# Reordering the setup of a fused long-convolution and SwiGLU kernel, gating its weight loads, and splitting a pair of transposes

## The chip, the cores and the metric

The kernel runs on one core of one Trainium2 chip. The metric is the device time of one execution in microseconds (us); lower is better. The profile is one execution recorded by the hardware profiler; its span is a little shorter than the device time (346.7 us against a median of 349.8 us for the kernel before). PE is the TensorE matmul engine, DVE is VectorE, ACT is ScalarE, POOL is GpSimd, SP issues the DMAs (46 of 48 in the trace of the kernel before).

## The reference, cut to what matters

```python
# x: [1, 2048, 640] bf16.  State space of 192 complex modes per channel; F = 1536
h  = x + A(layernorm(x))             # A: long convolution + skip
h2 = h + B(layernorm(h))             # B: SwiGLU

def A(u):                            # per channel d
    K[d, l] = Re sum_n C[d,n] * exp(dt[d] * A[d,n] * l) * dt[d] * B[d,n]
    y = causal convolution of u with K along l (by FFT)
    return y + u * Dskip
def B(x):
    return (silu(x @ w1) * (x @ w3)) @ w2
```

The kernel builds the convolution filter for three chunks of channels (256, 256 and 128), transforms it with small matmuls, and then convolves block by block: 8 token chunks of 256 tokens, each with a forward transform, a product with the filter's spectrum `kf`, and an inverse transform, followed by the SwiGLU.

## The kernel before

The kernel asks for a manual schedule (`tc.manual_schedule()`), and in its traces each engine's instructions stand in the order in which the Python code issues them: that order is the schedule. The setup has, for each channel chunk h, two tables `at` and `bt` (ACT computes sines and exponentials, DVE multiplies them up), a product `k_mm` of the two on PE, its drain `k_evac` on ACT, and a transform `k_dft` on PE, whose result ACT copies to `kf` (for the last chunk ACT and DVE):

```python
    def k_dft(h, kc):                      # 256 small matmuls, each with its own weight load
        pp = [ps2("g"), ps2("g")]
        for i in range(II):                # 16
            for f in range(NFT):           # 4
                for blk in range(4):
                    ...
                    T.matmul(ob, lhsT=wt[...], rhs=rb, ...)
        return pp
    ...
    pb = k_dft(0, kc)
    kf_evac(0, pb, "SSSS")                 # ACT
    for ig, st in zip(IGS, stg):
        b_mul(1, bt1, "sin", ig, st)       # DVE
    zs2 = z_sin(2)                         # ACT: 6 sines
    bt2 = b_tile(2)
    b_first(2, bt2, "sin")                 # ACT: 30 sines
    stg = [b_rest(2, bt2, "exp", ig) for ig in IGS]    # ACT: 15 exponentials
    ...                                    # DVE: a_chain(2), b_mul(2)
    warm(14, last_a(1, at1))               # PE: matmuls whose result nobody reads
    warm(10, last_b(1, bt1, 1))
    for b in range(nb[1]):                 # 4 blocks
        pk = k_mm(1, at1, bt1, kc, b)      # PE
        k_evac(1, pk, kc, b)               # ACT: behind all of chunk 2's sines and exponentials
    ...
    nc.sync.dma_start(out=w1sb[:], ...)    # 1.97 MB each, issued as soon as their space is free
    nc.sync.dma_start(out=w3sb[:], ...)
    pb = k_dft(1, kc)
    kf_evac(1, pb, "SSSS")
    inverse_table()                        # 8 transposes on PE, then a copy to gt on DVE
    warm(8, last_b(2, bt2, 0))
    ...                                    # k_mm(2), k_evac(2)
    lst[0] = ln1_stats(0, V)               # DVE: mean, variance, 1/sqrt by Newton steps
    ulns[0] = ln1_apply(0, lst[0])
    lst[1] = ln1_stats(1, G)               # the Newton steps on POOL
    for f in range(NFT):
        fwd_evac(0, f, fwd_mm(ulns[0], f)) # forward transform of token chunk 0 -> vt
    pb = k_dft(2, kc)
    ...                                    # DVE: skip(0), apply(1), stats(2), skip(1), stats(3)
    kf_evac(2, pb, "SVSV")
```

The loop over token chunks, with `gu` a gate/up pair of matmul groups (20 matmuls, six times a pass):

```python
        gu(c, 4)
        if n1:
            tp = ps2("d", BF16)
            for k in range(2):
                tr_mm(c + 1, k, tp)        # 5 transposes on PE into PSUM tile tp
                tr_evac(c + 1, k, tp)      # ACT copies them to xt; PE's second half waits for it
        run(pr, 1)
        gu(c, 5)
        run(pr, 1)
        po = out_mm(c, 0)
        ...
```

Of the kernel before, what the change touches and what calls it, by code (L numbers as in the profile page):

```python
# [14 lines left out]
NFT = 4  # L15
# [13 lines left out]
def kernel(  # L29
# [105 lines left out]
    def inverse_table():  # L135
        tp = ps2("d", BF16)
        for i in range(NFT):
            for kt in range(2):
                T.transpose(out=tp[:, 0, i * TB + kt * P:i * TB + kt * P + P], in_=ft[:, kt, i * P:(i + 1) * P], identity=ident[:])
        V.tensor_copy(out=gt[:], in_=tp[:, 0, :].rearrange("p (i t) -> p i t", i=NFT))  # L140

    dtl = kp.tile([P, D], BF16, name="dtl")
    S.activation(out=dtl[:], in_=ldb[:], func=ACT.Exp)
# [96 lines left out]
    def b_nsin(h, i, dst):  # L240
        S.activation(out=dst, in_=grp(h, 1), func=ACT.Sin, scale=-float(i))  # L241

    def b_first(h, bt, kind):
        bv = b_view(h, bt)
        for i in range(1, II):
            if kind == "exp":
                b_exp(h, i, bv[:, 0, :, i, :])
            else:
                b_cos(h, i, bv[:, 0, :, i, :])
                b_nsin(h, i, bv[:, 1, :, i, :])  # L250
# [113 lines left out]
    def run(gen, n=None):  # L364
        r = None
        while n is None or n > 0:
            try:
                r = next(gen)
            except StopIteration:
                break  # L370
            if n is not None:
                n -= 1
        return r

    def rstd(v, n, eng):
        va = small.tile([P, 2], F32, name="va")
        ta = small.tile([P, 2], F32, name="ta")
        rs = small.tile([P, 2], F32, name="rs")
        u, t, r = va[:, 0:n], ta[:, 0:n], rs[:, 0:n]
        V.tensor_scalar(out=u, in0=v, scalar1=EPS, scalar2=None, op0=ALU.add)  # L380
        V.tensor_single_scalar(out=t.bitcast(I32), in_=u.bitcast(I32), scalar=1, op=ALU.arith_shift_right)
        V.tensor_scalar(out=r.bitcast(I32), in0=t.bitcast(I32), scalar1=-1.0, scalar2=float(0x5F3759DF), op0=ALU.mult, op1=ALU.add)  # L382
        for _ in range(2):
            eng.tensor_tensor(out=t, in0=r, in1=r, op=ALU.mult)  # L384
            eng.tensor_tensor(out=t, in0=t, in1=u, op=ALU.mult)
            eng.tensor_scalar(out=t, in0=t, scalar1=-0.5, scalar2=1.5, op0=ALU.mult, op1=ALU.add)
            eng.tensor_tensor(out=r, in0=r, in1=t, op=ALU.mult)
        return rs

    def bn(mv, k, src):  # L390
        st = small.tile([P, 2, V.BN_STATS_DIM], F32, name="st")
        for q in range(2):
            V.bn_stats(out=st[:, q, :], in_=src[:, q * (D // 2):(q + 1) * (D // 2)])  # L393
        V.bn_aggr(out=mv[:, k, :], in_=st[:])

    def ln1_stats(c, eng):
        mv = small.tile([P, 2, 2], F32, name="mv")
        for k in range(2):
            bn(mv, k, xs[:, 2 * c + k, :])
        return mv, rstd(mv[:, :, 1], 2, eng)  # L400

    def ln1_apply(c, stats):
        mv, rs = stats
        uln = vp.tile([P, 2, D], BF16, name="uln", bufs=2)
        for k in range(2):
            V.tensor_scalar(out=uln[:, k, :], in0=xs[:, 2 * c + k, :], scalar1=mv[:, k, 0:1], scalar2=rs[:, k:k + 1],
                            op0=ALU.subtract, op1=ALU.mult)
        return uln

# [4 lines left out]

    vts = {}

    def fwd_mm(uln, f):
        pv = ps2()
        for k in range(2):
            for q in range(2):  # L420
                T.matmul(pv[:, q, 0:D // 2], lhsT=ft[:, k, f * P:(f + 1) * P],  # L421
                         rhs=uln[:, k, q * (D // 2):(q + 1) * (D // 2)], start=(k == 0), stop=(k == 1))
        return pv

    def fwd_evac(c, f, pv):
        if f == 0:
            vts[c] = vp.tile([P, 2, 2, D], BF16, name="vt", bufs=4)
        S.copy(out=vts[c][:, f // 2, f % 2, :].rearrange("p (q d) -> p q d", q=2), in_=pv[:, :, 0:D // 2])  # L428

    w_mul(0, 0)  # L430
    alpha(0)
# [43 lines left out]
    z_mul(1, zs1, ze1)  # L475
    run(a_chain(1, at1, zs1))
    pb = k_dft(0, kc)
    kf_evac(0, pb, "SSSS")
    for ig, st in zip(IGS, stg):
        b_mul(1, bt1, "sin", ig, st)  # L480
    zs2 = z_sin(2)
    bt2 = b_tile(2)
    b_first(2, bt2, "sin")
    stg = [b_rest(2, bt2, "exp", ig) for ig in IGS]
    z_mul(2, zs2, ze2)
    at2 = kp.tile([P, 2 * JJ * CWM], BF16, name="at", bufs=1)
    V.tensor_copy(out=a_view(2, at2)[:, :, :, 0, :], in_=wl2[:].rearrange("p a (q c) -> p a q c", c=2))
    run(a_chain(2, at2, zs2))
    for ig, st in zip(IGS, stg):
        b_mul(2, bt2, "exp", ig, st)  # L490
    warm(14, last_a(1, at1))
    warm(10, last_b(1, bt1, 1))
    kc = kp.tile([P, II * 4 * 2 * (max(CHUNKS) // 8)], BF16, name="kc")
    for b in range(nb[1]):
        pk = k_mm(1, at1, bt1, kc, b)
        k_evac(1, pk, kc, b)
    bctx.close()
    wts = ctx.enter_context(tc.tile_pool(name="wts", bufs=1, side="right", reuse_waits="tile"))
    w1sb = wts.tile([P, DT, F], BF16, name="w1sb")
    w3sb = wts.tile([P, DT, F], BF16, name="w3sb")  # L500
    vp = ctx.enter_context(tc.tile_pool(name="vp", bufs=4, side="right", reuse_waits="tile"))
    nc.sync.dma_start(out=w1sb[:], in_=B_w1.rearrange("(s p) f -> p s f", p=P))
    nc.sync.dma_start(out=w3sb[:], in_=B_w3.rearrange("(s p) f -> p s f", p=P))
    pb = k_dft(1, kc)
    kf_evac(1, pb, "SSSS")
    inverse_table()
    kc = kp.tile([P, II * 4 * 2 * (max(CHUNKS) // 8)], BF16, name="kc")
    warm(8, last_b(2, bt2, 0))
    for b in range(nb[2]):
        pk = k_mm(2, at2, bt2, kc, b)  # L510
        k_evac(2, pk, kc, b)
    lst, ulns = {}, {}
    lst[0] = ln1_stats(0, V)
    ulns[0] = ln1_apply(0, lst[0])
    lst[1] = ln1_stats(1, G)
    for f in range(NFT):
        fwd_evac(0, f, fwd_mm(ulns[0], f))
    pb = k_dft(2, kc)
    skip(0, ulns[0])
    ulns[1] = ln1_apply(1, lst[1])  # L520
    lst[2] = ln1_stats(2, G)
    skip(1, ulns[1])
    lst[3] = ln1_stats(3, G)
    kf_evac(2, pb, "SVSV")
    kctx.close()
    if dbg and "kf" in dbg:
        nc.sync.dma_start(out=dbg["kf"], in_=kf[:])

    mp = ctx.enter_context(tc.tile_pool(name="mp", bufs=1, side="left", reuse_waits="tile"))
    w2sb = mp.tile([P, FT, D], BF16, name="w2sb")  # L530
    nc.sync.dma_start(out=w2sb[:], in_=B_w2.rearrange("(s p) d -> p s d", p=P))
    zz, xx, hst, xls, xts = {}, {}, {}, {}, {}

    def product(c):
# [3 lines left out]
        x = z if c == 0 else mp.tile([P, 2, 2, D], BF16, name="xf", bufs=2)  # L538
        zz[c], xx[c] = z, x
        zp = zz.pop(c - 1, None)  # L540
        pstr = z[:].ap[0][0]
        n = D // 2
        for q in range(2):
            r = slice(q * n, (q + 1) * n)
# [10 lines left out]
                                        op=(ALU.subtract if a == e else ALU.add))  # L555
            yield

    def inv_mm(c, k):
        py = ps2()
        for f in range(NFT):  # L560
            for q in range(2):
                T.matmul(py[:, q, 0:D // 2], lhsT=gt[:, f, k * P:(k + 1) * P],  # L562
                         rhs=xx[c][:, f // 2, f % 2, q * (D // 2):(q + 1) * (D // 2)], start=(f == 0), stop=(f == NFT - 1))
        return py

    def h_add(c, k, py):
        hv = xs[:, 2 * c + k, :].rearrange("p (q d) -> p q d", q=2)
# [50 lines left out]
                        in1=xs[:, tt, :].rearrange("p (q d) -> p q d", q=2), op=ALU.add)  # L618
        nc.sync.dma_start(out=out_view[:, tt, :], in_=ot[:])

    run(product(0))
    for f in range(NFT):
        fwd_evac(1, f, fwd_mm(ulns[1], f))
    py = [inv_mm(0, 0), inv_mm(0, 1)]
    for k in range(2):
        h_add(0, k, py[k])
        rs = rstd(hst[0][:, k:k + 1, 1], 1, V)
        ln2_apply(0, k, hst[0], rs, 0)
        tp = ps2("d", BF16)
        tr_mm(0, k, tp)  # L630
        tr_evac(0, k, tp)
        if k == 0:
            ulns[2] = ln1_apply(2, lst[2])
            for f in range(NFT):
                fwd_evac(2, f, fwd_mm(ulns[2], f))
    run(product(1))
    skip(2, ulns[2])

    for c in range(NC):
        n1, n2, n3, n4 = (c + 1 < NC), (c + 2 < NC), (c + 3 < NC), (c + 4 < NC)  # L640
        if n3:
            ulns[c + 3] = ln1_apply(c + 3, lst[c + 3])
        gu(c, 0)
        if n1:
            p0 = inv_mm(c + 1, 0)
            h_add(c + 1, 0, p0)
        gu(c, 1)
        if n1:
            p1 = inv_mm(c + 1, 1)
            h_add(c + 1, 1, p1)  # L650
            rs = rstd(hst[c + 1][:, :, 1], 2, G)
        gu(c, 2)
        if n3:
            for f in (0, 1):
                fwd_evac(c + 3, f, fwd_mm(ulns[c + 3], f))
            skip(c + 3, ulns[c + 3])
        gu(c, 3)
        if n1:
            for k in range(2):
                ln2_apply(c + 1, k, hst[c + 1], rs, k)  # L660
        if n3:
            for f in (2, 3):
                fwd_evac(c + 3, f, fwd_mm(ulns[c + 3], f))
        pr = product(c + 2) if n2 else iter(())
        if n4:
# [19 lines left out]
_INS = ['A_u', 'A_A_re', 'A_A_im', 'A_B_re', 'A_B_im', 'A_C_re', 'A_C_im', 'A_log_dt', 'A_Dskip', 'B_x', 'B_w1', 'B_w3', 'B_w2']  # L685
# [26 lines left out]
```

## Time and profile before

| | before |
|---|---|
| median, range | 349.8 us, 348.0 to 352.0 (16 runs) |
| span of the profiled run | 346.7 us |
| busy PE / DVE / ACT / POOL | 74 / 78 / 43 / 11 % |

Those shares are averages over two quite different stretches. The first view is the table of busy time by stretch, with the cuts at 99.2 us (DVE has finished the last table, `bt2`) and at 151.3 us (start of the second gate/up group). Its columns are the stretch, its length, busy time of each engine (with instruction counts), the mean granted PE clock as a share of full speed, the DMA share and GB/s.

```profile
0.00:99.20 99.20, 39.72 (x620) 27.86 (x621) 93.85 (x166) 84.27 (x191) 3.27 (x14) 0.86 0.26 70
99.20:151.30 52.10, 31.53 (x695) 20.84 (x695) 37.46 (x115) 16.24 (x27) 9.45 (x24) 0.74 0.33 115
151.30:346.70 195.40, 184.95 (x1580) 151.60 (x1577) 140.40 (x309) 49.31 (x81) 26.58 (x88) 1.00 0.04 15
```

Up to 99.2 us DVE is busy for 93.9 us of 99.2: it bounds that part, and the change leaves its work there alone. From 151.3 us PE is busy for 185 of 195 us at full clock: it bounds the loop. Between lie 52.1 us in which no engine is the limit: DVE works for 37.5 us of it, PE for 31.5, and the PE clock averages 0.74. That stretch is where a better order can win.

The next view is the chain of waits in that stretch: start, length, and the work or wait that held up everything behind it.

```profile
97.98 0.24 PE ps L308 x8
...
98.24 1.50 ACT kc L326 x2
...
99.79 2.16 PE ps L336 x242
101.95 4.90 issue
106.85 0.39 PE ps L336 x14
107.24 0.98 PE ps L139 x8
...
108.24 0.69 DVE gt L140
108.93 0.80 DVE st L393 x2
```

DVE could have gone on at 99.24 us. It waits until 108.24 because its next instruction, the copy of `gt`, hangs on PE's `k_dft(1)`, which begins only at 99.79 and stops for 4.90 us in the middle ("issue": the engine waited for nothing that the trace records). The list of DVE's waits from 49 to 135 us (engine, line, what it waited for; total us, times, longest) shows that wait as the largest:

```profile
DVE gt L140 <- PE ps L139: 9.0, 1, 9.0
DVE uln L406 <- POOL rs L387: 1.7, 1, 1.7
DVE xs L568 <- PE ps L562: 1.7, 1, 1.7
```

What is PE doing in those 4.90 us? The DMA view of 104 to 106 us shows two queues at work (packets, MB, share of the 16 DMA engines' time):

```profile
q1 hardware_dynamic: 267, 0.77, 99.8%
q8 instruction: 1, 0.02, 3.3%
```

q8, which the profile calls "instruction", moves packets of 16 KB (22 packets, 0.36 MB in the whole run), and they keep PE's pace: in the loop eleven of them begin from 156.28 us up to, but not including, the one at 328.10, and PE starts 2820 matmuls and weight loads in that time, 256 for each packet. At 256 each, 22 packets make 5632 instructions, and PE has 5784 matmuls and weight loads. From this the author takes q8 as the fetch of PE's instructions. In this trace one such packet begins between 104 and 106 us (at 104.29, by the packet records of the trace, and it ends at 105.35), and none between 98 and 104, while the loads of `w1` and `w3`, issued at 98.28 and 98.71 us, keep the DMA engines nearly full.

In the loop the wait between the two halves of the transpose shows in PE's timeline (start, length, line, operation, operands, count; in brackets the idle time before it and what ended it):

```profile
188.96 0.44 PE L581 MATMUL ps<-ident,xl 128*128 128x128 bf16 x5
190.39 0.44 PE L581 MATMUL ps<-ident,xl 128*128 128x128 bf16 x5 [0.99 <-DVE ta L381]
190.66 1.25 PE L597 MATMUL ps<-xt,w1sb 128*128 128x256 bf16 x10
191.75 1.25 PE L597 MATMUL ps<-xt,w3sb 128*128 128x256 bf16 x10
192.84 6.68 PE L610 MATMUL ps<-w2sb,hm 128*128 128x320 bf16 x48
```

PE stands still for 0.99 us while ACT empties the first half (the trace names a DVE instruction as the one that ended the wait in this pass, and ACT's `xt` copy in four of the seven; ACT's copy ends at the same moment, and `xt` is what the code makes it wait for).

### The profile page before, as it was taken

What the parts mean: (1) busy time and instruction counts of PE and PEld (TensorE: products, weight loads), DVE (VectorE), ACT (ScalarE), POOL (GpSimd) and SP (SyncE); (2) the same over time, 40 slices, a digit from 0 to 9 for tenths busy, and PEclk for the clock granted to TensorE, in tenths of its full rate; (3) what the DMA queues carried; (4) which work ended last, traced back from release to release, by engine and by line L of the source; (5) the groups of instructions that cost most, each with busy time, mean ns of one, the idle gap of its engine ahead of it and who ended that gap; (6) DMA issues with size and microseconds to landing.
All of it is one profiled execution on the core that took longest, in us unless ns stands there. A gap on an engine that the chain in (4) does not pass through costs nothing.

```text
span 346.7 us, 7002 instructions
## 1 busy us (share of the span) xinstructions
PE 256.2 (74%) x2892; PEld 200.3 (58%) x2892; DVE 271.7 (78%) x588; ACT 149.8 (43%) x298; POOL 39.3 (11%) x126
## 2 busy tenths in 40 slices
PE   3303056377256655788998998998998998998995
PEld 1201025254254432467787787787787787787884
DVE  6899999999944797999888798798796685873331
ACT  2999999939931630425115115116015023022120
POOL 2000000000000352003303203203202001010000
PEclk9999999558786965699999999999999999999999
DMA  5823800000057070000000000000000000100101
GB/s 158 265 89 92 182 0 2 0 6 1 0 185 275 2 227 5 0 1 2 20 20 2 19 21 0 22 19 2 21 19 2 20 21 0 41 2 0 40 0 38
DMA packets 10655, 15.74 MB, mean 45 GB/s; under 512 B 1536, under 2 KB 9216, under 8 KB 10496
## 3 DMA queue, kind: packets, MB, share of 16 engines
q1 hardware_dynamic: 10336, 15.11, 14.0%
q8 instruction: 22, 0.36, 0.4%
q10 hardware_dynamic: 288, 0.20, 0.2%
q14 instruction: 9, 0.07, 0.1%
HBM read 12.42 MB, written 2.88 MB: 44 GB/s over the span
## 4 chain that ended last, share of the span: by engine, by line
PE 55%; DVE 24%; ACT 13%; issue 4%; DMA 1%; POOL 1%; SPq 0%; DVEq 0%
PE ps L597 28%; PE ps L610 15%; PE ps L562 5%; DVE st L393 4%; ACT bt L241 2%; ACT kc L326 2%; PE ps L421 2%; DVE at L291 2%; DVE tt L293 2%; DVE at L296 2%; PE ps L308 2%; PE ps L336 2%; ACT bt L238 1%; ACT stg L238 1%; ACT sg L602 1%
## 5 line engine op out<-in xcount | busy, mean ns | idle before, releaser
L602 ACT ACTIVATE sg<-ps 128x512 bf16<-128x512 f32 x48 | 28.7, 597 | 133.5 <-PE ps L597 133.5
L597 PE MATMUL ps<-xt,w1sb 128*128 128x256 bf16 x480 | 60.2, 273 | 1.1 <-ACT xt L586 1.1
L597 PE MATMUL ps<-xt,w3sb 128*128 128x256 bf16 x480 | 60.2, 273 | 0.0
L603 DVE TENSOR_TENSOR hm<-sg,ps 128x512 bf16<-128x512 bf16 x48 | 32.9, 686 | 33.4 <-ACT sg L602 33.0
L610 PE MATMUL ps<-w2sb,hm 128*128 128x320 bf16 x384 | 53.5, 299 | 0.0
L597 PEld LDWEIGHTS <-w1sb 128*128 128x128 bf16 x480 | 46.7, 98 | 8.1 <-issue 1.2
L597 PEld LDWEIGHTS <-w3sb 128*128 128x128 bf16 x480 | 47.0, 98 | 5.4
L610 PEld LDWEIGHTS <-hm 128*128 128x128 bf16 x384 | 37.6, 98 | 14.2
L384 POOL TENSOR_TENSOR ta<-rs 128x2 f32<-128x2 f32 x28 | 8.9, 317 | 203.1 <-DVE rs L382 202.0
L393 DVE BATCH_NORM_STATS2 st<-xs 128x6 f32<-128x320 bf16 x64 | 27.9, 478 | 0.5
L308 PE MATMUL ps<-bt,at 128*128 128x128 bf16 (+1 forms) x320 | 18.8, 239 | 10.6 <-ACT kc L326 10.5
L617 DVE TENSOR_TENSOR ot<-ps,xs 128x640 bf16<-128x640 f32 x16 | 13.2, 825 | 15.7 <-PE ps L610 15.7
L421 PE MATMUL ps<-uln,ft 128*128 128x320 bf16 x128 | 23.2, 332 | 2.0 <-ACT kc L326 0.8
L308 PEld LDWEIGHTS <-at 128*128 128x128 bf16 (+1 forms) x320 | 16.5, 106 | 13.5 <-issue 11.4
L428 ACT CAST vt<-ps 128x640 bf16<-128x640 f32 x32 | 21.0, 694 | 4.2 <-PE ps L421 4.2
L562 PEld LDWEIGHTS <-gt 128*128 128x128 bf16 x128 | 13.1, 103 | 13.4 <-DVE z L549 4.5
L241 ACT ACTIVATE bt<-alp 128x384 bf16<-128x384 f32 (+1 forms) x45 | 20.6, 458 | 0.0
L356 PEld LDWEIGHTS <-ident 128*128 128x128 bf16 x56 | 7.0, 132 | 23.4 <-DVE at L296 12.0
L291 DVE TENSOR_TENSOR at<-at,zs 128x1536 bf16<-128x1536 bf16 (+3 forms) x30 | 20.2, 675 | 0.1
L293 DVE TENSOR_TENSOR tt<-at,zs 128x1536 bf16<-128x1536 bf16 (+3 forms) x30 | 20.2, 673 | 0.0
L336 PE MATMUL ps<-kc,wt 32*128 32x64 bf16 (+1 forms) x768 | 8.8, 204 | 14.5 <-issue 8.4
L296 DVE TENSOR_TENSOR at<-at,tt 128x1536 bf16<-128x1536 bf16 (+3 forms) x30 | 19.1, 678 | 0.5
(96 smaller groups left out, 371.4 us busy)
## 6 DMA issues: line engine op xcount, KB each, us to landing
xs<-in_A_u_dram SPq DMA_DIRECT2D x4, 640.0 KB, 6.3
out_dram<-ot SPq DMA_DIRECT2D x16, 160.0 KB, 1.8
wt<-ftd SPq DMA_DIRECT2D x4, 512.0 KB, 7.7
w1sb<-in_B_w_dram SPq DMA_DIRECT2D x1, 1920.0 KB, 8.6
w3sb<-in_B_w_dram SPq DMA_DIRECT2D x1, 1920.0 KB, 13.1
w2sb<-in_B_w_dram SPq DMA_DIRECT2D x1, 1920.0 KB, 9.5
ftd<-ft SPq DMA_DIRECT2D x1, 256.0 KB, 2.1
par_ar<-in_A_A_re_dram SPq DMA_DIRECT2D x2, 96.0 KB, 3.8
```

What stands on the lines that cost most here:

```text
L241: S.activation(out=dst, in_=grp(h, 1), func=ACT.Sin, scale=-float(i))
L291: V.tensor_tensor(out=av[:, part, :, o0:o0 + w, :], in0=src, in1=z4[:, 0].broadcast_to([P, cw // 2, w, 2]), op=ALU.mult)
L293: V.tensor_tensor(out=tv[:, part], in0=src, in1=z4[:, 1].broadcast_to([P, cw // 2, w, 2]), op=ALU.mult)
L296: V.tensor_tensor(out=dst, in0=dst, in1=tv[:, 1 - part], op=(ALU.add if part else ALU.subtract))
L308: T.matmul(pk[:, half, gi * P:(gi + 1) * P], lhsT=at[r, c], rhs=bt[r, c], start=first, stop=last, tile_position=((r.start, 0) if n1 else N ...
L393: V.bn_stats(out=st[:, q, :], in_=src[:, q * (D // 2):(q + 1) * (D // 2)])
L421: T.matmul(pv[:, q, 0:D // 2], lhsT=ft[:, k, f * P:(f + 1) * P], rhs=uln[:, k, q * (D // 2):(q + 1) * (D // 2)], start=(k == 0), stop=(k = ...
L562: T.matmul(py[:, q, 0:D // 2], lhsT=gt[:, f, k * P:(k + 1) * P], rhs=xx[c][:, f // 2, f % 2, q * (D // 2):(q + 1) * (D // 2)], start=(f == ...
L597: T.matmul(pg[:, b, u * TB:(u + 1) * TB], lhsT=w[:, kt, fb * P:(fb + 1) * P], rhs=xts[c][:, kt, :], start=(kt == 0), stop=(kt == DT - 1))
L602: S.activation(out=sg[:], in_=pg[:, 0, :], func=ACT.Silu)
L603: V.tensor_tensor(out=hms[c][:, 2 * fp:2 * fp + 2, :], in0=sg[:].rearrange("p (u t) -> p u t", u=2), in1=pg[:, 1, :].rearrange("p (u t) -> ...
L610: T.matmul(po[:, q, 0:D // 2], lhsT=hms[c][:, fb, k * P:(k + 1) * P], rhs=w2sb[:, fb, q * (D // 2):(q + 1) * (D // 2)], start=(fb == 0), s ...
```

## The change

Its intent is to shorten the stretch from 99 to 151 us, and to fill the wait in the loop. It has six parts:

1. ACT's order: chunk 2's sines run while PE is in `k_dft(0)`, and chunk 2's exponentials alternate with the drains of chunk 1.
2. The loads of w1 and w3 are gated: SP first issues a tiny DMA out of the last `kf`, so that they start after the last `k_dft`.
3. The transposes go on either side of the sixth gate/up group.
4. DVE's layernorm work is reordered: statistics of token chunks 0 and 1 together with one shared 1/sqrt; the two halves of chunk 0 share one in the second layernorm too; the forward transforms run two chunks ahead instead of three, so one moves from the setup into the loop.
5. Fewer warm-up matmuls (30 instead of 56).
6. `gt`, and the whole of the last `kf`, is copied by ACT instead of DVE; the forward transform is split by halves of the channels, and the inverse one too, so that products can begin earlier; ACT's first Silu stands ahead of the loop, and with it the table load of 1.28 us that the trace shows before it.

The diff, cut to its core:

```diff
@@ inverse_table
-        V.tensor_copy(out=gt[:], in_=...)
+        S.copy(out=gt[:], in_=...)
@@ setup
     pb = k_dft(0, kc)
-    kf_evac(0, pb, "SSSS")
     ...
     zs2 = z_sin(2)
     bt2 = b_tile(2)
-    b_first(2, bt2, "sin")
-    stg = [b_rest(2, bt2, "exp", ig) for ig in IGS]
+    b_first(2, bt2, "sin", 1, 8)
+    kf_evac(0, pb, "SSSS")
+    b_first(2, bt2, "sin", 8, II)
     ...
-    warm(14, last_a(1, at1))
-    warm(10, last_b(1, bt1, 1))
+    warm(6, last_b(1, bt1, 1))
+    stg = []
     for b in range(nb[1]):
         pk = k_mm(1, at1, bt1, kc, b)
+        if b < len(IGS):
+            stg.append(b_rest(2, bt2, "exp", IGS[b]))
         k_evac(1, pk, kc, b)
     ...
-    nc.sync.dma_start(out=w1sb[:], ...)
-    nc.sync.dma_start(out=w3sb[:], ...)
     pb = k_dft(1, kc)
     ...
-    warm(8, last_b(2, bt2, 0))
     ...
-    lst[0] = ln1_stats(0, V); ulns[0] = ln1_apply(0, lst[0]); lst[1] = ln1_stats(1, G)
-    for f in range(NFT):
-        fwd_evac(0, f, fwd_mm(ulns[0], f))
     pb = k_dft(2, kc)
-    ...   # skip(0), apply(1), stats(2), skip(1), stats(3)
-    kf_evac(2, pb, "SVSV")
+    mv, ulns = ln1_stats((0, 1)), {}
+    rs = rstd(mv[:, :, 1], 4, V)
+    ...   # apply(0), apply(1), stats(2), skip(0), skip(1)
+    kf_evac(2, pb, "SSSS")
+    for q, part in ((0, 0), (0, 1), (1, 0), (1, 1)):
+        fwd(0, ulns[0], q, part)
+    warms = small.tile([P, 1], F32, name="warms")
+    S.activation(out=warms[:], in_=pit[:], func=ACT.Silu)
     ...
+    gate(kf[0:1, 1, 1, D - 64:D])          # SP: tiny DMA that waits for the last kf
+    nc.sync.dma_start(out=w1sb[:], ...)
+    nc.sync.dma_start(out=w3sb[:], ...)
     nc.sync.dma_start(out=w2sb[:], ...)
@@ loop
         gu(c, 4)
         if n1:
             tp = ps2("d", BF16)
-            for k in range(2):
-                tr_mm(c + 1, k, tp)
-                tr_evac(c + 1, k, tp)
+            tr_mm(c + 1, 0, tp)
+            tr_evac(c + 1, 0, tp)
         run(pr, 1)
         gu(c, 5)
+        if n1:
+            tr_mm(c + 1, 1, tp)
+            tr_evac(c + 1, 1, tp)
         run(pr, 1)
     ...   # ln1_apply and the forward transform of chunk c + 2 instead of c + 3
```

More of the change, by code (lines that the diff above doesn't have):

```diff
@@ L139, in inverse_table @@
                 T.transpose(out=tp[:, 0, i * TB + kt * P:i * TB + kt * P + P], in_=ft[:, kt, i * P:(i + 1) * P], identity=ident[:])
-        V.tensor_copy(out=gt[:], in_=tp[:, 0, :].rearrange("p (i t) -> p i t", i=NFT))
+        S.copy(out=gt[:], in_=tp[:, 0, :].rearrange("p (i t) -> p i t", i=NFT))
     dtl = kp.tile([P, D], BF16, name="dtl")
@@ L241, in b_nsin, with b_first @@
         S.activation(out=dst, in_=grp(h, 1), func=ACT.Sin, scale=-float(i))
-    def b_first(h, bt, kind):
+    def b_first(h, bt, kind, i0=1, i1=II):
         bv = b_view(h, bt)
-        for i in range(1, II):
+        for i in range(i0, i1):
             if kind == "exp":
@@ L375, in rstd @@
     def rstd(v, n, eng):
-        va = small.tile([P, 2], F32, name="va")
-        ta = small.tile([P, 2], F32, name="ta")
-        rs = small.tile([P, 2], F32, name="rs")
+        va = small.tile([P, 4], F32, name="va")
+        ta = small.tile([P, 4], F32, name="ta")
+        rs = small.tile([P, 4], F32, name="rs")
         u, t, r = va[:, 0:n], ta[:, 0:n], rs[:, 0:n]
@@ L394, in bn, with ln1_stats, ln1_apply @@
         V.bn_aggr(out=mv[:, k, :], in_=st[:])
-    def ln1_stats(c, eng):
-        mv = small.tile([P, 2, 2], F32, name="mv")
-        for k in range(2):
-            bn(mv, k, xs[:, 2 * c + k, :])
-        return mv, rstd(mv[:, :, 1], 2, eng)
-    def ln1_apply(c, stats):
-        mv, rs = stats
-        uln = vp.tile([P, 2, D], BF16, name="uln", bufs=2)
-        for k in range(2):
-            V.tensor_scalar(out=uln[:, k, :], in0=xs[:, 2 * c + k, :], scalar1=mv[:, k, 0:1], scalar2=rs[:, k:k + 1],
+    def ln1_stats(cs):
+        mv = small.tile([P, 4, 2], F32, name="mv")
+        for i, c in enumerate(cs):
+            for k in range(2):
+                bn(mv, 2 * i + k, xs[:, 2 * c + k, :])
+        return mv
+    def ln1_apply(c, mv, rs, o):
+        uln = vp.tile([P, 2, D], BF16, name="uln", bufs=3)
+        for k in range(2):
+            V.tensor_scalar(out=uln[:, k, :], in0=xs[:, 2 * c + k, :], scalar1=mv[:, o + k, 0:1], scalar2=rs[:, o + k:o + k + 1],
                             op0=ALU.subtract, op1=ALU.mult)
@@ L415, with fwd, gate @@
     vts = {}
-    def fwd_mm(uln, f):
+    def fwd(c, uln, q, part):
+        if (q, part) == (0, 0):
+            vts[c] = vp.tile([P, 2, 2, D], BF16, name="vt", bufs=3)
+        r = slice(q * (D // 2), (q + 1) * (D // 2))
         pv = ps2()
-        for k in range(2):
-            for q in range(2):
-                T.matmul(pv[:, q, 0:D // 2], lhsT=ft[:, k, f * P:(f + 1) * P],
-                         rhs=uln[:, k, q * (D // 2):(q + 1) * (D // 2)], start=(k == 0), stop=(k == 1))
-        return pv
-    def fwd_evac(c, f, pv):
-        if f == 0:
-            vts[c] = vp.tile([P, 2, 2, D], BF16, name="vt", bufs=4)
-        S.copy(out=vts[c][:, f // 2, f % 2, :].rearrange("p (q d) -> p q d", q=2), in_=pv[:, :, 0:D // 2])
+        for e in range(2):
+            f = 2 * part + e
+            for k in range(2):
+                T.matmul(pv[:, e, 0:D // 2], lhsT=ft[:, k, f * P:(f + 1) * P], rhs=uln[:, k, r], start=(k == 0), stop=(k == 1))
+        S.copy(out=vts[c][:, part, :, r], in_=pv[:, :, 0:D // 2])
+    def gate(src):
+        nc.sync.dma_start(out=gated[:], in_=src)
     w_mul(0, 0)
@@ L488 @@
     run(a_chain(2, at2, zs2))
+    warm(6, last_b(1, bt1, 1))
+    kc = kp.tile([P, II * 4 * 2 * (max(CHUNKS) // 8)], BF16, name="kc")
+    stg = []
+    for b in range(nb[1]):
+        pk = k_mm(1, at1, bt1, kc, b)
+        if b < len(IGS):
+            stg.append(b_rest(2, bt2, "exp", IGS[b]))
+        k_evac(1, pk, kc, b)
     for ig, st in zip(IGS, stg):
         b_mul(2, bt2, "exp", ig, st)
-    warm(14, last_a(1, at1))
-    warm(10, last_b(1, bt1, 1))
-    kc = kp.tile([P, II * 4 * 2 * (max(CHUNKS) // 8)], BF16, name="kc")
-    for b in range(nb[1]):
-        pk = k_mm(1, at1, bt1, kc, b)
-        k_evac(1, pk, kc, b)
     bctx.close()
@@ L501 @@
     vp = ctx.enter_context(tc.tile_pool(name="vp", bufs=4, side="right", reuse_waits="tile"))
-    nc.sync.dma_start(out=w1sb[:], in_=B_w1.rearrange("(s p) f -> p s f", p=P))
-    nc.sync.dma_start(out=w3sb[:], in_=B_w3.rearrange("(s p) f -> p s f", p=P))
     pb = k_dft(1, kc)
@@ L511 @@
         k_evac(2, pk, kc, b)
-    lst, ulns = {}, {}
-    lst[0] = ln1_stats(0, V)
-    ulns[0] = ln1_apply(0, lst[0])
-    lst[1] = ln1_stats(1, G)
-    for f in range(NFT):
-        fwd_evac(0, f, fwd_mm(ulns[0], f))
-    pb = k_dft(2, kc)
-    skip(0, ulns[0])
-    ulns[1] = ln1_apply(1, lst[1])
-    lst[2] = ln1_stats(2, G)
-    skip(1, ulns[1])
-    lst[3] = ln1_stats(3, G)
-    kf_evac(2, pb, "SVSV")
+    pb = k_dft(2, kc)
+    mv, ulns = ln1_stats((0, 1)), {}
+    rs = rstd(mv[:, :, 1], 4, V)
+    for c in range(2):
+        ulns[c] = ln1_apply(c, mv, rs, 2 * c)
+    mv = ln1_stats((2,))
+    st1 = {2: (mv, rstd(mv[:, :, 1][:, 0:2], 2, G))}
+    for c in range(2):
+        skip(c, ulns[c])
+    kf_evac(2, pb, "SSSS")
[3 more added lines that the diff above has]
+    S.activation(out=warms[:], in_=pit[:], func=ACT.Silu)
     kctx.close()
@@ L530 @@
     w2sb = mp.tile([P, FT, D], BF16, name="w2sb")
+    gated = dram.tile([1, 64], BF16, name="gated")
+    gate(kf[0:1, 1, 1, D - 64:D])
+    nc.sync.dma_start(out=w1sb[:], in_=B_w1.rearrange("(s p) f -> p s f", p=P))
+    nc.sync.dma_start(out=w3sb[:], in_=B_w3.rearrange("(s p) f -> p s f", p=P))
     nc.sync.dma_start(out=w2sb[:], in_=B_w2.rearrange("(s p) d -> p s d", p=P))
@@ L540, in product @@
         zp = zz.pop(c - 1, None)
-        pstr = z[:].ap[0][0]
         n = D // 2
@@ L556, in product, with inv_mm @@
             yield
-    def inv_mm(c, k):
-        py = ps2()
+    def inv_mm(c, k, q, py):
         for f in range(NFT):
-            for q in range(2):
-                T.matmul(py[:, q, 0:D // 2], lhsT=gt[:, f, k * P:(k + 1) * P],
-                         rhs=xx[c][:, f // 2, f % 2, q * (D // 2):(q + 1) * (D // 2)], start=(f == 0), stop=(f == NFT - 1))
-        return py
+            T.matmul(py[:, q, 0:D // 2], lhsT=gt[:, f, k * P:(k + 1) * P],
+                     rhs=xx[c][:, f // 2, f % 2, q * (D // 2):(q + 1) * (D // 2)], start=(f == 0), stop=(f == NFT - 1))
     def h_add(c, k, py):
@@ L619, in out_add @@
         nc.sync.dma_start(out=out_view[:, tt, :], in_=ot[:])
-    run(product(0))
-    for f in range(NFT):
-        fwd_evac(1, f, fwd_mm(ulns[1], f))
-    py = [inv_mm(0, 0), inv_mm(0, 1)]
+    p0, p1 = product(0), [ps2(), ps2()]
+    run(p0, 2)
     for k in range(2):
-        h_add(0, k, py[k])
-        rs = rstd(hst[0][:, k:k + 1, 1], 1, V)
-        ln2_apply(0, k, hst[0], rs, 0)
-        tp = ps2("d", BF16)
+        inv_mm(0, k, 0, p1[k])
+    run(p0)
+    for k in range(2):
+        inv_mm(0, k, 1, p1[k])
+    for k in range(2):
+        h_add(0, k, p1[k])
+    for q, part in ((0, 0), (0, 1), (1, 0), (1, 1)):
+        fwd(1, ulns[1], q, part)
+    r0 = rstd(hst[0][:, :, 1], 2, V)
+    tp = ps2("d", BF16)
+    for k in range(2):
+        ln2_apply(0, k, hst[0], r0, k)
         tr_mm(0, k, tp)
         tr_evac(0, k, tp)
-        if k == 0:
-            ulns[2] = ln1_apply(2, lst[2])
-            for f in range(NFT):
-                fwd_evac(2, f, fwd_mm(ulns[2], f))
     run(product(1))
-    skip(2, ulns[2])
     for c in range(NC):
-        n1, n2, n3, n4 = (c + 1 < NC), (c + 2 < NC), (c + 3 < NC), (c + 4 < NC)
-        if n3:
-            ulns[c + 3] = ln1_apply(c + 3, lst[c + 3])
-        gu(c, 0)
-        if n1:
-            p0 = inv_mm(c + 1, 0)
-            h_add(c + 1, 0, p0)
-        gu(c, 1)
-        if n1:
-            p1 = inv_mm(c + 1, 1)
-            h_add(c + 1, 1, p1)
+        n1, n2, n3 = (c + 1 < NC), (c + 2 < NC), (c + 3 < NC)
+        if n2:
+            ulns[c + 2] = ln1_apply(c + 2, *st1.pop(c + 2), 0)
+        for k in range(2):
+            gu(c, k)
+            if n1:
+                py = ps2()
+                for q in range(2):
+                    inv_mm(c + 1, k, q, py)
+                h_add(c + 1, k, py)
+        if n1:
             rs = rstd(hst[c + 1][:, :, 1], 2, G)
         gu(c, 2)
-        if n3:
-            for f in (0, 1):
-                fwd_evac(c + 3, f, fwd_mm(ulns[c + 3], f))
-            skip(c + 3, ulns[c + 3])
+        if n2:
+            for q, part in ((0, 0), (0, 1)):
+                fwd(c + 2, ulns[c + 2], q, part)
+            skip(c + 2, ulns[c + 2])
         gu(c, 3)
@@ L660 @@
                 ln2_apply(c + 1, k, hst[c + 1], rs, k)
+        if n2:
+            for q, part in ((1, 0), (1, 1)):
+                fwd(c + 2, ulns[c + 2], q, part)
+        pr = product(c + 2) if n2 else iter(())
         if n3:
-            for f in (2, 3):
-                fwd_evac(c + 3, f, fwd_mm(ulns[c + 3], f))
-        pr = product(c + 2) if n2 else iter(())
-        if n4:
-            lst[c + 4] = ln1_stats(c + 4, G)
+            mv = ln1_stats((c + 3,))
+            st1[c + 3] = (mv, rstd(mv[:, :, 1][:, 0:2], 2, G))
         gu(c, 4)
@@ L669 @@
             tp = ps2("d", BF16)
-            for k in range(2):
-                tr_mm(c + 1, k, tp)
-                tr_evac(c + 1, k, tp)
+            tr_mm(c + 1, 0, tp)
+            tr_evac(c + 1, 0, tp)
         run(pr, 1)
         gu(c, 5)
+        if n1:
+            tr_mm(c + 1, 1, tp)
+            tr_evac(c + 1, 1, tp)
         run(pr, 1)
```

## The prediction

It was written before the changed kernel had run.

> **What bounds the kernel now.** The timeline by engine shows two regimes. Up to 151.3 us (start of the second gate/up group) the kernel is latency-bound: VectorE (DVE) is busy without a break from 49 to 99.2 us (building the at and bt tables), then PE, ACT and DVE take turns; the PE clock is near half speed in much of 60 to 145 us (windows). From 151.3 us to the end PE runs almost back to back (19.0 of every 20 us): 25.68 us per token chunk, of which 0.99 us is a wait for the xt copy between the two transposes.
>
> **The setup.** In the chain of waits, DVE finishes bt2 at 99.2 us, but PE reaches chunk 2's matmuls only at 111.0, because ACT drains chunk 1 late (k_evac begins at 91.8, behind all of chunk 2's sines and exponentials), k_dft(1) starts only at 99.8, and it stops for 4.9 us ("issue", 101.95 to 106.85). I read that stop as instruction fetch behind the 3.9 MB of w1/w3, issued at 98.3 us: [...] the trace has an instruction queue of 16 KB packets, and the other two k_dft stop 1.6 and 1.95 us with no bulk transfer under way.
>
> The change starts chunk 2's sines while k_dft(0) runs (ACT idled 5.5 us there), interleaves chunk 1's drains with the exponentials (k_evac(1) done near 93.5 instead of 99.7), drops 26 of 56 warm-up matmuls in this stretch, sends the gt copy to ACT, and gates the weight loads behind the last kf. My walk along the engines' orders, with the trace's durations: k_dft(1) 93.5 to about 98; k_mm(2) about 99.5 to 103; k_dft(2) done near 108.5 (was 122.2); vt(0) ready near 112.
>
> DVE, meanwhile, no longer waits: from 99.2 us statistics of chunks 0 and 1 (4.2), one shared rstd (2.2), four applies (1.5), statistics of chunk 2 (2.7), two skips (3.3): 113.1 us. Product(0) 4.9, last inverse matmuls 1.3, two h_add 4.0, rstd 2.1, ln2 0.8: 126.1 (was 144.2). Product(1) 6.7, then the second gate/up group at about 133.7 instead of 151.3: **-17.6 us**. Early PE delays of up to some 2 us hide behind DVE. Weights issued near 110 should have landed by 119, 124 and 129 us (w1, w3, w2; estimates from 8.6 and 13.1 us before), ahead of the first gate/up group near 128.
>
> **The loop.** One forward transform moves into it (chunk 5's pass): **+2.2 us**. Splitting the transposes around the sixth gate/up group removes the 0.99 us wait in seven passes: **-7 us**. DVE has about 22.3 us of work in a 24.7 us pass, so PE should stay the limit.
>
> Sum -22.4: **327.5 us**, range 323.5 to 332. Chances: faster by over 2% 0.96, within 2% 0.03, slower 0.01.
>
> **What would show it.** k_dft(1) with a stop of about 2 us, not 4.9; k_dft(2) ending before 110; DVE without idle from 49 to about 117; second gate/up group near 133.7; pass period about 24.6; the xt wait gone.
>
> **What would make it wrong.** Weights late, so that the first gate/up group waits; instruction fetch of PE, ACT or DVE stuck behind 5.9 MB of weights; fewer warm-ups leaving PE at half clock in k_mm(1), k_mm(2) or the first gate/up group (each a few us); DVE, now about 90% busy in the loop, delaying PE each pass.

That the instruction fetch of ACT or DVE could stick behind the weights is not shown: in the kernel after, neither has an "issue" wait from 111 to 130 us, while 5.9 MB were moved.

## The result

| | before | after |
|---|---|---|
| median | 349.8 us (16 runs) | 324.6 us (11 runs) |
| range | 348.0 to 352.0 | 323.8 to 325.7 |
| span of the profiled run | 346.7 us | 321.7 us |

The ratio is 0.9286, with a 95% interval of 0.9261 to 0.9312: the kernel is 7% faster. Here and below a ratio is the mean time of one kernel's fast runs over that of the other's in the same rounds, so it is not quite the ratio of the medians quoted beside it.

The table by stretch for the kernel after, with the second cut at 132.0 us, where its second gate/up group starts:

```profile
0.00:99.20 99.20, 39.97 (x866) 28.70 (x866) 93.93 (x167) 85.72 (x196) 3.27 (x14) 0.86 0.26 70
99.20:132.00 32.80, 21.96 (x406) 15.56 (x407) 30.76 (x86) 13.46 (x22) 5.16 (x8) 0.79 0.51 182
132.00:321.70 189.70, 186.04 (x1595) 152.93 (x1593) 143.27 (x320) 51.01 (x85) 31.32 (x96) 1.00 0.04 15
```

The first stretch is unchanged. The middle one shrank from 52.1 to 32.8 us, and the loop from 195.4 to 189.7 us. In the middle stretch DVE worked 37.5 us and idled 14.6 us before; now it works 30.8 us and idles 2.0 us. So of the 19.3 us gained there, 12.6 us is idle time of DVE that is gone, and 6.7 us is DVE work that is gone from that place. In the loop DVE gained 2.9 us of work (143.3 us against 140.4), which PE's work hides. DVE now works almost without a pause from 49 us to the loop; its waits in 49 to 135 us come down to this one:

```profile
DVE xs L569 <- PE ps L564: 0.5, 1, 0.5
```

PE's timeline of the setup in the kernel after:

```profile
93.75 2.28 PE L336 MATMUL ps<-kc,wt 32*128 32x64 bf16 x256 [2.34 <-ACT kc L326]
95.96 0.40 PE L139 MATMUL ps<-ident,ft 128*128 128x128 bf16 x4
98.72 0.40 PE L139 MATMUL ps<-ident,ft 128*128 128x128 bf16 x4 [2.37 <-issue]
99.23 4.71 PE L308 MATMUL ps<-bt,at 128*128 128x128 bf16 x64
105.47 1.70 PE L336 MATMUL ps<-kc,wt 32*128 32x32 bf16 x187 [1.54 <-ACT kc L326]
109.14 0.73 PE L336 MATMUL ps<-kc,wt 32*128 32x32 bf16 x69 [1.97 <-issue]
109.80 3.91 PE L425 MATMUL ps<-uln,ft 128*128 128x320 bf16 x16
```

`k_dft(1)` starts at 93.75 us instead of 99.79. The stop is still there, now at the transposes behind it, but it takes 2.37 us instead of 4.90. `k_dft(2)` ends at 109.87 us; before, it ended at 122.2.

In the loop, PE's timeline around the transposes answers to the one shown of before:

```profile
168.55 0.44 PE L582 MATMUL ps<-ident,xl 128*128 128x128 bf16 x5
168.82 1.25 PE L598 MATMUL ps<-xt,w1sb 128*128 128x256 bf16 x10
169.92 1.25 PE L598 MATMUL ps<-xt,w3sb 128*128 128x256 bf16 x10
171.01 0.44 PE L582 MATMUL ps<-ident,xl 128*128 128x128 bf16 x5
171.29 6.68 PE L611 MATMUL ps<-w2sb,hm 128*128 128x320 bf16 x48
```

The wait is gone. A pass from one output projection to the next takes 24.52 us (171.29 to 195.81), where it took 25.68 us.

### The profile page after: what moved, and what is told of

Same layout as the page of the kernel before. It is cut to its first block, busy times and chain, and to the rows that moved or that the text cites. A ratio compares the mean times of both kernels' runs of the same rounds, so it can differ in the third digit from the quotient of the medians.

```text
span 321.7 us, 6931 instructions
## 1 busy us (share of the span) xinstructions
PE 248.0 (77%) x2866; PEld 197.2 (61%) x2866; DVE 268.0 (83%) x571; ACT 150.2 (47%) x302; POOL 39.8 (12%) x118
## 3 DMA queue, kind: packets, MB, share of 16 engines
q1 hardware_dynamic: 10338, 15.11, 15.1%
## 4 chain that ended last, share of the span: by engine, by line
PE 60%; DVE 34%; ACT 2%; issue 2%; DMA 1%; SPq 0%; DVEq 0%
PE ps L598 33%; PE ps L611 16%; DVE at L291 6%; DVE at L296 6%; DVE tt L293 6%; PE ps L564 5%; PE ps L425 4%; DVE bt L269 3%; DVE bt L268 3%; DVE st L393 2%; PE ps L582 1%; DVE alp L172 1%; DMA par_br<-in_A_B_re_dram 1%; DVE zs L215 1%; DVE w L187 1%
## 5 line engine op out<-in xcount | busy, mean ns | idle before, releaser
L598 PE MATMUL ps<-xt,w1sb 128*128 128x256 bf16 x480 | 61.3, 276 | 0.8 <-ACT xt L587 0.8
L384 POOL TENSOR_TENSOR ta<-rs 128x2 f32<-128x2 f32 x26 | 9.6, 368 | 177.7 <-DVE rs L382 176.7
L308 PE MATMUL ps<-bt,at 128*128 128x128 bf16 (+1 forms) x320 | 20.6, 251 | 5.5 <-ACT kc L326 5.3
L308 PEld LDWEIGHTS <-at 128*128 128x128 bf16 (+1 forms) x320 | 18.0, 112 | 9.0 <-issue 7.1
L425 PE MATMUL ps<-uln,ft 128*128 128x320 bf16 x128 | 21.6, 315 | 1.4 <-ACT vt L426 1.0
L152 PE MATMUL ps<-ident,wdn 128*128 128x128 bf16 x10 | 2.9, 288 | 19.9 <-DVE wdn L188 19.9
L564 PE MATMUL ps<-xf,gt 128*128 128x320 bf16 x112 | 17.6, 299 | 0.0
## 6 DMA issues: line engine op xcount, KB each, us to landing
w2sb<-in_B_w_dram SPq DMA_DIRECT2D x1, 1920.0 KB, 16.7
```

Of the source, the lines that this page charges most:

```text
L308: T.matmul(pk[:, half, gi * P:(gi + 1) * P], lhsT=at[r, c], rhs=bt[r, c], start=first, stop=last, tile_position=((r.start, 0) if n1 else N ...
L425: T.matmul(pv[:, e, 0:D // 2], lhsT=ft[:, k, f * P:(f + 1) * P], rhs=uln[:, k, r], start=(k == 0), stop=(k == 1))
L564: T.matmul(py[:, q, 0:D // 2], lhsT=gt[:, f, k * P:(k + 1) * P], rhs=xx[c][:, f // 2, f % 2, q * (D // 2):(q + 1) * (D // 2)], start=(f == ...
L598: T.matmul(pg[:, b, u * TB:(u + 1) * TB], lhsT=w[:, kt, fb * P:(fb + 1) * P], rhs=xts[c][:, kt, :], start=(kt == 0), stop=(kt == DT - 1))
```

## The experiments

### Parts of the change alone, added to the kernel before

**Only the gate.** The loads of w1 and w3 are moved behind the last `kf`, as in the change:

```diff
-    nc.sync.dma_start(out=w1sb[:], ...)     # ahead of k_dft(1)
-    nc.sync.dma_start(out=w3sb[:], ...)
     pb = k_dft(1, kc)
     ...
     w2sb = mp.tile(...)
+    nc.sync.dma_start(out=gated[:], in_=kf[0:1, 1, 1, D - 64:D])
+    nc.sync.dma_start(out=w1sb[:], ...)
+    nc.sync.dma_start(out=w3sb[:], ...)
     nc.sync.dma_start(out=w2sb[:], ...)
```

> The kernel before, with only the weight loads of w1 and w3 moved behind the last kf (the gate). Theory (the 4.9 us stop of PE in k_dft(1) is instruction fetch queued behind the weights): the stop shrinks to about 2 us, everything after shifts by it, about 347 us (-2.5 to -3). Rival (the stop has another cause, or the later weights cost as much): the stop stays near 4.9 us, about 350 us.

Measured: median 348.1 us, ratio 0.9933 (0.9847 to 1.002). The time alone does not settle it, since the interval holds 1. The list of PE's waits in 100 to 107 us does:

```profile
PE ps L336 <- issue: 2.5, 1, 2.5
```

The stop fell from 4.9 to 2.5 us, and only the loads had moved. The expected gain of 2.5 to 3 us is close to the 2.3 us that the ratio gives (0.0067 of 350.2), but only as a point estimate.

**Only the split of the transposes.** The loop part of the diff above, in the kernel before.

> The kernel before, with only the two transposes of a pass put on either side of the sixth gate/up group. Theory (PE bounds the pass, the wait between the transposes is pure loss): 7 passes times 0.99 to 1.15 us, about 342 us. Rival (DVE, with 22.3 us of work in a 24.6 us pass, becomes the limit): 345 to 349 us.

Measured: median 342.2 us, ratio 0.9786 (0.9726 to 0.9846), that is -7.5 us. The passes take 24.52 us in its trace as well (167.78 to 192.30 us between output projections). The first theory holds; DVE does not become the limit.

**Only ACT's order** (part 1 of the list, with the warm-ups kept).

```diff
     pb = k_dft(0, kc)
-    kf_evac(0, pb, "SSSS")
     ...
-    b_first(2, bt2, "sin")
-    stg = [b_rest(2, bt2, "exp", ig) for ig in IGS]
+    b_first(2, bt2, "sin", 1, 8)
+    kf_evac(0, pb, "SSSS")
+    b_first(2, bt2, "sin", 8, II)
     ...
     for b in range(nb[1]):
         pk = k_mm(1, at1, bt1, kc, b)
+        if b < len(IGS):
+            stg.append(b_rest(2, bt2, "exp", IGS[b]))
         k_evac(1, pk, kc, b)
```

> The kernel before, with only ACT's order in the setup changed (chunk 2's sines during k_dft(0), chunk 1's drains between the exponentials). Theory (PE's late k_dft(1) holds back everything after it): k_dft(1) starts near 93.5 instead of 99.8 us, still stops some 5 us behind the weights, about 344 us. Rival (DVE is busy until 99.2 us anyway, so an earlier k_dft(1) buys little): 348 to 350 us.

Measured: median 342.9 us, ratio 0.9807 (0.974 to 0.9873), -6.8 us. `k_dft(1)` starts at 93.40 us and stops for 4.54 us behind the weights, which are issued at 91.12 us here. DVE's wait for `gt` falls from 9.0 to 2.4 us,

```profile
DVE gt L140 <- PE ps L139: 2.4, 1, 2.4
```

and that difference of 6.6 us is about the gain. The theory holds.

**Gate, split and ACT's order together.**

> The kernel before with gate, split and ACT order together, without the new order of DVE's layernorm work, the moved forward transform, the gt copy on ACT and the fewer warm-ups. Theory (parts mostly add): -3 -8 -6, about 333 us, so that the rest, 8 to 9 us, belongs to the new DVE order. Rival (these three are the whole gain): about 325 us.

Measured: median 332.5 us, ratio 0.9507 (0.9441 to 0.9572), -17.3 us; the three single gains sum to -16.6 us. They add, and they are not the whole. The kernel after is a further 7.7 us faster (0.9507 less 0.9286, times 350 us). The table by stretch of this run, cut at its second gate/up group (142.3 us), shows where those are:

```profile
99.20:142.30 43.10, 28.07 (x428) 18.12 (x426) 37.43 (x115) 14.58 (x22) 9.45 (x24) 0.73 0.39 138
```

DVE works 37.4 us in this stretch, as in the kernel before, and idles 5.7 us. The kernel after has 30.8 us of work and 2.0 us of idle time in it. The stretch is 10.3 us shorter there (142.3 to 132.0 us), and 2.2 us of that is paid back in the loop by the forward transform that moved into it: 8.1 us, against the 7.7 us measured. DVE's waits in 49 to 135 us of this run are

```profile
DVE uln L406 <- POOL rs L387: 1.7, 1, 1.7
DVE xs L573 <- PE ps L567: 1.7, 1, 1.7
```

The first, for a 1/sqrt on POOL, is gone in the kernel after; the second, for the last inverse matmuls, is 0.5 us there. So most of the rest belongs to part 4, the DVE work that was shared (one 1/sqrt for two chunks or two halves) or moved into the loop: of the 6.7 us of DVE work that is gone only 0.7 us is the `gt` copy and 0.5 us the `kf` copy of part 6, and the wait for POOL adds 1.7 us, some 7 of the 10.3 us by this estimate. The shorter wait for the inverse matmuls goes with their split in part 6 and with PE's pace there: 4.16 us for 15 of them in this run, as in the kernel before at a granted clock of 0.50, and 1.38 us for eight at 1.00 in the kernel after. This is the difference of two runs and their traces; neither part 4 nor the splits and the early Silu table of part 6 were run alone, so their shares are not shown by an experiment.

### Parts of the change taken back, from the kernel after

**Weights early again.** w1 and w3 issued ahead of `k_dft(1)`, without the gate.

> The kernel after, with w1 and w3 issued early again (no gate), so that they run during k_dft(1). Theory (instruction fetch behind the weights, and PE's path to vt(0) has no slack in the kernel after): PE's stop after k_dft(1) grows from 2.4 to some 5 us, and the time by about 2 us, 326 to 327.5 us. Rival (bulk loads do not touch PE, or DVE hides the delay): 324.6 us, within 0.5.

Measured: median 327.6 us, ratio 0.9367 (0.9318 to 0.9416), +2.8 us over the kernel after (one of the four runs, the profiled one with 325.4 us, lies within the range of the kernel after, so the size is loose). Its waits of PE in 93 to 101 us and of DVE in 49 to 135 us, the largest of each:

```profile
PE ps L139 <- issue: 3.5, 1, 3.5
```

```profile
DVE z L546 <- ACT vt L426: 1.8, 1, 1.8
```

The stop grew from 2.4 to 3.5 us, less than the 5 us expected, and `k_dft(1)` itself took 2.86 us instead of 2.28, so the stop alone is not the whole delay: from the start of `k_dft(1)` to the end of the stop it is 6.93 us instead of 4.97. The `k_mm(2)` behind them starts at 100.67 instead of 99.23 us, and DVE now waits 1.8 us for the forward transform's result. The rival, that DVE hides such a delay, falls.

**ACT's order taken back.**

> The kernel after, with ACT's order in the setup as before. Theory (PE's path through k_dft(1), k_mm(2), k_dft(2) to vt(0) has no slack): k_dft(1) starts near 99.8 us, about +5.5 us, 330 us. Rival (DVE bounds the setup, PE's path has slack): 324.6 to 326 us.

Measured: median 331.4 us, ratio 0.9479 (0.9439 to 0.9519), +6.7 us. `k_dft(1)` starts at 101.47 us in its trace, 7.7 us later than in the kernel after, and DVE's largest wait is

```profile
DVE z L548 <- ACT vt L426: 7.1, 1, 7.1
```

The rival (slack on PE's path) falls here too.

**Transposes together again.**

> The kernel after, with the two transposes of a pass together again. Theory (1.15 us in each of 7 passes, as the passes of 25.68 and 24.52 us show): about +8 us, 332.6 us. Rival (something else shortened the pass): under 328 us.

Measured: median 332.9 us, ratio 0.9525 (0.9495 to 0.9556), +8.4 us. The pass is back at 25.67 us (149.16 to 174.83 us) and the wait of 0.99 us stands in all seven passes. The theory holds: this is the largest of the parts taken back.

**Warm-ups back.** 14, 10 and 8 warm-up matmuls instead of 6.

```diff
-    warm(6, last_b(1, bt1, 1))
+    warm(14, last_a(1, at1))
+    warm(10, last_b(1, bt1, 1))
     ...
     inverse_table()
+    warm(8, last_b(2, bt2, 0))
```

> The kernel after, with all 32 warm-up matmuls of this stretch instead of 6. Theory (the warm-ups cost PE as much as they win in clock): the 8 ahead of chunk 2's matmuls take about 3 us at half clock and win 1.5 us back; 325 to 327 us. Rival (the missing warm-ups cost the kernel after time, since k_mm(2) ran at half clock): 322 to 324 us.

Measured: median 325.3 us, ratio 0.9299 (0.9261 to 0.9337), not to be told from the kernel after. PE's timeline around `k_mm(2)` in this run:

```profile
98.59 3.15 PE L356 MATMUL ps<-bt,ident 128*128 128x480 bf16 x8
101.53 3.52 PE L308 MATMUL ps<-bt,at 128*128 128x128 bf16 x64
```

The eight warm-ups delay `k_mm(2)` to 101.53 us and it then takes 3.52 us; without them it starts at 99.23 us and takes 4.71 us, with a granted clock of 0.50 from 99.36 to 102.78 us. It ends at 105.05 instead of 103.94 us. The warm-ups are not worth their time, as expected, but the effect on the whole is below what these runs resolve.

**gt on DVE again.**

> The kernel after, with the copy of gt back on DVE. Theory (DVE is on the critical chain from 49 us on, and the copy takes it 0.69 us): +0.5 to +1 us, at the edge of what the timing resolves. Rival: no change.

Measured: median 325.0 us, ratio 0.9285 (0.9233 to 0.9336). No change was resolved. In its trace DVE takes 0.69 us for the copy and reaches the first product at 113.72 instead of 112.87 us, as the theory wants; the time neither supports nor refutes 0.5 to 1 us.

### Looking for more: are there two critical chains?

In the kernel after, DVE reaches the first product, which needs the forward transform `vt(0)`, at 112.87 us. The first lines are DVE's last skip and that product; the second fence is ACT's timeline, whose second entry completes the half of `vt(0)` that the product reads:

```profile
112.07 0.82 DVE L413 TENSOR_TENSOR xs<-pd,xs 128x1280 bf16<-128x1280 bf16 x1
112.87 0.82 DVE L551 TENSOR_TENSOR z<-vt,kf 128x1280 bf16<-128x1280 bf16 x1
```

```profile
109.92 0.77 ACT L348 CAST kf<-ps 128x128 bf16<-128x128 f32 x4 [4.50 <-PE ps L336]
111.08 0.69 ACT L426 CAST vt<-ps 128x640 bf16<-128x640 f32 x1 [0.39 <-PE ps L425]
112.15 0.69 ACT L426 CAST vt<-ps 128x640 bf16<-128x640 f32 x1 [0.37 <-PE ps L425]
113.20 1.29 ACT L426 CAST vt<-ps 128x640 bf16<-128x640 f32 x2 [0.36 <-PE ps L425]
```

The half is complete at 112.84 us (112.15 plus 0.69). The two chains meet within 0.03 us. Three runs try to shorten one, the other and both. The first puts the forward transform into `k_dft(2)`, just ahead of the stop:

```diff
-    def k_dft(h, kc):
+    def k_dft(h, kc, mid=None):
         ...
         for i in range(II):
             ...
+            if mid is not None and i == 9:
+                mid()                      # the 16 matmuls of fwd(0) and their drains
```

> The kernel after, with the forward transform of chunk 0 issued inside k_dft(2) (after 10 of its 16 steps), where PE stops 2 us for its instructions. Theory (in the kernel after, DVE reaches product(0) at 112.87 us and vt(0)'s first half is ready at 112.84, so both chains are critical and shortening one gains nothing): vt(0) ready 1.5 to 2 us earlier, time unchanged, 324 to 325 us. Rival (PE's path alone is critical): about 323 us.

Measured: median 325.2 us, ratio 0.9278 (0.9233 to 0.9323). The first half of `vt(0)` was ready at 108.87 us, 4 us earlier (1.5 to 2 were expected), and the stop in `k_dft(2)` vanished; DVE reached the product at 112.91 us and the time did not move. The theory holds. The second defers DVE's skip of chunk 1:

```diff
-    for c in range(2):
-        skip(c, ulns[c])
+    skip(0, ulns[0])
     ...
             gu(c, k)
+            if c == 0 and k == 0:
+                skip(1, ulns[1])
```

> The kernel after, with the skip of chunk 1 (1.65 us of DVE) moved from ahead of product(0) into the first pass of the loop. Theory (two equal chains): DVE waits 1.6 us for vt(0), time unchanged, 324 to 325 us. Rival (DVE alone is critical): about 323 us.

Measured: median 323.9 us, ratio 0.9257 (0.921 to 0.9304), not resolved from the kernel after. DVE waited for `vt`, as expected, but 0.7 us and not 1.6: in the profiled run PE's granted clock happened to be 1.00 in `k_mm(2)` (100 to 104 us), where the kernel after has 0.50 up to 102.78 us, and `vt` came 0.9 us earlier. Both together:

> Both of these together. Theory (two equal chains, both shortened): product(0) starts about 1.6 us earlier, and the first pass of the loop has enough DVE slack for the skip: 322.5 to 323.5 us. Rival (one of the two alone holds the time, or the loop's DVE has no room for the skip): the same as the better of the two alone.

Measured: median 323.6 us, ratio 0.9240 (0.9197 to 0.9282). The product starts at 112.26 us, only 0.6 us earlier, because a third chain is there: PE takes 3.80 us for the forward transform ahead of the rest of `k_dft(2)` (3.91 us in the kernel after, with a granted clock of 0.50 up to 113.02 us; in the loop, at 1.00, twice 1.25 us), so the last `kf` is late.

```profile
DVE z L555 <- ACT kf L350: 1.1, 1, 1.1
```

Its median is the lowest of all, but the interval overlaps that of the kernel after. It is not shown to be faster, and no version was found that is.

### All runs

| run | median us | ratio to before | |
|---|---|---|---|
| before | 349.8 | 1 | |
| only the gate | 348.1 | 0.9933 | unclear in time, stop 4.9 to 2.5 us |
| only the split | 342.2 | 0.9786 | -7.5 us |
| only ACT's order | 342.9 | 0.9807 | -6.8 us |
| these three | 332.5 | 0.9507 | -17.3 us |
| **after** | 324.6 | 0.9286 | -25.0 us |
| after, weights early | 327.6 | 0.9367 | +2.8 us over after |
| after, ACT's order back | 331.4 | 0.9479 | +6.7 us |
| after, transposes together | 332.9 | 0.9525 | +8.4 us |
| after, warm-ups back | 325.3 | 0.9299 | same |
| after, gt on DVE | 325.0 | 0.9285 | same |
| after, forward transform in k_dft(2) | 325.2 | 0.9278 | same |
| after, skip(1) later | 323.9 | 0.9257 | not resolved |
| after, both | 323.6 | 0.9240 | not resolved |

The two ways of taking the change apart agree within the noise, which is 1 to 3 us on each of these figures: the gate is worth 2.3 (not resolved by itself) or 2.8 us, ACT's order 6.8 or 6.7, the split 7.5 or 8.4.

## Why the prediction was right

The measured 324.6 us lies inside the predicted range of 323.5 to 332, near its lower end, 2.9 us below the predicted 327.5. Point by point:

- **The setup, -17.6 us predicted.** Measured 19.3 us (151.3 to 132.0 us). DVE's sequence came out nearly as added up: product(0) at 112.87 us for a predicted 113.1, both `ln2` applies done at 125.07 for 126.1. The largest mis-sized term is the last inverse matmuls, 1.3 us predicted and 0.5 us measured (DVE's wait of 0.52 us up to 118.29 us; PE's clock was 1.00 there, and 0.50 in the kernel before). The second gate/up group then followed product(1) after 0.2 us, for which the prediction had left 0.9.
- **The stop of k_dft(1), about 2 us instead of 4.9.** Measured 2.37 us. That the weights were the cause is shown from both sides: taking them away from the kernel before cut the stop to 2.5 us, and putting them back into the kernel after lengthened it to 3.5 us. In all 14 traces, from the start of `k_dft(1)` to the end of the stop it is 6.7 to 7.1 us in the four with the weights under way and 4.2 to 5.1 us in the ten without.
- **The loop, +2.2 and -7 us.** Measured 195.4 to 189.7 us, -5.7 us, for -4.8 predicted. The split was mis-sized: it saves 1.15 us in a pass (25.68 to 24.52), not the 0.99 us that the trace marks as idle, because the tail of the first transposes is covered by the sixth gate/up group too (from the first transposes to PE's next work it is 0.27 us instead of 1.43, in the two timelines above). Seven times 1.15 is 8.1 us; 2.2 less 8.1 is -5.9.
- **DVE does not limit the loop.** Right: the passes are 24.52 us from the second to the sixth, and taking the split back cost 8.4 us.
- **Weights in time.** Right: issued at 111.2, 111.7 and 112.4 us, they landed 7.5, 12.0 and 16.7 us later, at 118.7, 123.7 and 129.1 us; the first gate/up group started at 127.3 us and needs only the first two.
- **"Early PE delays of up to some 2 us hide behind DVE" was wrong.** The trace had no such slack: `vt(0)`'s first half was ready 0.03 us before DVE wanted it. The prediction put `k_dft(2)`'s end at 108.5 us; it was 109.87, mostly since `k_mm(2)` took 4.71 us, with a granted clock of 0.50 from 99.36 to 102.78 us. That this cost nothing was luck: the error on PE's side (`vt(0)` at 112.84 us for a predicted 112) just used up the time until DVE arrived, at 112.87 us. Weights early (+2.8 us, DVE waits 1.8 us) and ACT's order back (+6.7 us, DVE waits 7.1 us) show a delay of PE passing through to the end.
- **The half clock was a named risk, and it came.** `k_mm(2)` took 4.71 us (granted clock 0.50 from 99.36 to 102.78 us) where the kernel before took 3.16 (at 1.00), and the first gate/up group took 3.52 us (0.50 from 126.67 to 130.08 us) instead of 2.18 (at 1.00), to the start of the matmul after it. Putting the warm-ups back did not help: eight of them took 3.15 us and saved 1.2 us of `k_mm(2)`.

The stop deserves a second look, as it seems to come at odd places: after 138 matmuls in `k_dft(0)`, after 242 in `k_dft(1)`, after 145 in `k_dft(2)` of the kernel before. Counted by PE's matmuls in the trace (transposes and warm-ups among them), each with its weight load, there are 512 matmuls or 1024 instructions from the first stop to the second, and 255 or 510 from the second to the third; in the kernel after it is 512 and 255 again, though what stands at the stops differs (`k_dft(0)`, a transpose, `k_dft(2)`). In the loop PE starts 256 matmuls and weight loads for each packet of q8, as counted above; 1024 is 4 times 256, and 510 is two short of 2 times 256 (instructions that only wait are not in this count). The packets agree: in both traces the packet that ends the second stop is the fourth after the one that ends the first, and the one that ends the third is the second after that. `k_dft` goes through 256 instructions in 1.1 to 2 us (an estimate from 242 matmuls in 2.16 us and 138 in 2.05 us in the kernel before), where the loop takes 15.1 to 16.1 us from packet to packet; from 130 us on PE's waits show no such stop, before or after. That the stop is the wait for the next packet's instructions is the reading of these counts.

The stops also end with q8's packets: by the packet records, PE goes on 1.2 to 1.6 us after the end of one in all 40 stops of the 14 traces (1.37, 1.50 and 1.38 us in the kernel before). There are three stops in each trace, and two in the two runs with the forward transform inside `k_dft(2)`. A stop of 1.0 to 2.5 us stands even with no bulk transfer under way. The packet that ends the stop of `k_dft(0)` begins only 0.9 to 1.2 us after `k_dft(0)` has started (1.02 us in the kernel before), although PE had stood still for over 4 us before (4.43 us there). What the weights add is the time until the packet begins: in `k_dft(1)` it begins 4.4 to 4.6 us after the start with the weights under way (in the kernel before at 104.29 us for a start at 99.79), 1.9 to 2.5 us after it without them (in the kernel after at 95.85 for 93.75), and it then takes 0.9 to 1.4 us in either case. From 104 to 106 us of the kernel before the weights' queue q1 takes 99.8% of the 16 DMA engines' time; that the packet stood behind it there is the author's reading, as no view shows what a packet waits for.

As for the clock, the granted clock in 2 us windows of both traces is 0.50 or 1.00, apart from windows that hold a change, and by the clock records of the two traces the changes stand whole multiples of 3.41 us apart. What makes it fall is not shown. In the 3.41 us ahead of the fall at 104.01 us in the kernel before PE worked for 1.35 us, and ahead of the fall at 106.19 us in the kernel after for 1.87 us, while 1.61 us of work between 89.12 and 92.54 us left the clock of the kernel after at 1.00. So the busy time of such a stretch alone does not tell when the clock falls; what does stays open here.

## What to carry to other kernels

When the engines take turns, list for each of them when its next instruction could start and what it is waiting for; here the 9.0 us wait of DVE fell to 2.4 us by reordering ACT alone, two steps upstream, and no instruction became faster. Check which bulk loads run while an engine goes through hundreds of very short instructions: here PE's stop in `k_dft(1)` was 4.9 us with 3.9 MB of weights under way and 2.5 us with the loads moved, and in the kernel after 2.4 us, and 3.5 us with the loads put back. Before counting on slack, check how far apart the two chains arrive: here two chains met within 0.03 us, and shortening either one alone gained nothing that the runs resolve.
